# A short causal convolution ahead of a ReGLU feed-forward: VectorE's convolution lane works one unit ahead instead of two

## The chip, the cores and the metric

One NeuronCore of a Trainium2 chip runs one program. The metric is the device time of an execution in microseconds (us); lower is better.

## The reference

`x` is 8 batches x 4096 tokens x 192 channels. Each of 8 heads (24 channels each) has 7 taps, a softmax over `weight`. A causal convolution over the tokens with these taps is followed by a gated feed-forward layer with 1536 hidden columns:

```python
w = softmax(weight, axis=-1)                                  # 8 x 7
out = einsum('hk,bskhg->bshg', w, windows of 7 tokens of x)   # zeros ahead of token 0
x = out.reshape(B * S, 192)
return (maximum(x @ w_gate, 0) * (x @ w_val)) @ w_out         # 192 -> 1536 -> 192
```

## The kernel before

**Units.** Four pairs of batches (batch b and batch b + 4 lie as two streams of 64 rows on the 128 partitions) are cut into units of 1024 tokens: 16 units, `u` = 0 to 15, two windows of 512 tokens in each. For each unit TensorE runs the *gates* (`gate_val`, line 505): two windows, in each 12 slices of hidden columns, in each six pairs of 64-row matmuls. Per slice ScalarE makes the ReLU (line 516) and VectorE the product `hT` (line 517). Then it runs the *projection* (`project`): four pieces of 512 tokens times `Wo`, each copied out by ScalarE (line 573; the last piece of a unit is shared with VectorE) and stored by a DMA on SP's queue (line 574).

**Half passes.** In all units but unit 0 a piece is projected in two turns of `half_pass` (line 528), 48 matmuls of 64 rows each, two of them side by side in the array. The second turn adds into the banks of the first, with the row halves exchanged, so it may start only when the first is over. This is told through an empty instruction on SP:

```python
        if turn == 0:
            done = nc.sync.nop()
            tc.add_manual_dep(done.ins, mm.ins.name, SYNC, reason="first turn over")
```

The first matmul of the second turn waits for this nop (line 549 in the profile). The order of turns is (0,0) (1,0) (0,1) (2,0) (1,1) (3,0) (2,1) (3,1), written (piece, turn). Unit 0 uses `half_whole` (line 553) in place of it: 48 matmuls of 128 rows per piece, with no second turn and no nop.

**Where the convolution is done.** The gates read the convolved tokens `xc[u]`. Unit 0 comes from small TensorE matmuls (`conv_dense`). Unit 1 comes from `conv(2)` and `conv(3)`: eight matmuls with band matrices each, five ScalarE copies into `y` (line 373, `move`), and DMA transposes on SP into `xc[1]` (line 395), five per group. Units 2 to 15 come from the *lane*: `lane_load` (GpSimd's queue loads raw tokens into `x_e`), `lane_turn` (GpSimd copies to `x_p`, nine DMA transposes on SP make `x_r`, line 436), `lane_first` (ScalarE, tap 0, into `acc`, line 469), `lane_rest` (VectorE, taps 1 to 6 on the first 576 tokens, line 481; 18 instructions, the last three write `xc`), `product` (ScalarE line 452 and VectorE line 454, taps times the last 448 tokens) and `add` (GpSimd sums the products, line 458).

**Order.** The schedule is written by hand: each engine runs its instructions in program order. In round `u` of the main loop the lane of unit `u + 2` is turned on GpSimd and SP during the gates, taken by ScalarE and VectorE during the projection, and its sums are added by GpSimd in the next round. PSUM is a ring of four buffers of two banks.

**Start.** GpSimd's queue issues the weight loads, and GpSimd copies slices 2 to 5 of `Wg` and `Wv` to the other 64 partitions (`pool_halves`, line 180); then come the copy of `tap`, `lane_load(2)`, `load_x(2)`, the load of `Wo`, and in round 0 `lane_turn(2)` and `load_x(3)`.

Of the kernel before, what the change touches and what calls it, by code (L numbers as in the profile page):

```python
# [15 lines left out]
def kernel(  # L16
# [41 lines left out]
    second = [min(t, 2 * UNIT - SUB) for t in range(UNIT, 2 * UNIT, SUB)]  # L58
    GROUPS += [(0, second[:GSUB]), (0, second[GSUB:])]
# [3 lines left out]
    xpool = ctx.enter_context(tc.tile_pool(name="xpool", bufs=3))  # L63
# [3 lines left out]
    ypool = ctx.enter_context(tc.tile_pool(name="ypool", bufs=2))  # L67
# [7 lines left out]
    def load_x(g):  # L75


        bp, toks = GROUPS[g]
        xt = xpool.tile([128, GSUB, 2, D], F16, name="x_h")
        rows, step = (SUB, DSUB) if g < 2 else (128, SUB)  # L80
        for st in range(2):
            b = bp + NB * st
            last = toks[-1] - toks[-2] != step
            n_full = len(toks) - int(last)
            src = bass.AP(
                tensor=x.tensor,
                offset=x.offset + (b * S + toks[0] - PAD) * D,
                ap=[[D, rows], [step * D, n_full], [1, D]],
            )
            nc.gpsimd.dma_start(out=xt[0:rows, 0:n_full, st, :], in_=src)  # L90
            if last:
                nc.gpsimd.dma_start(
                    out=xt[0 : SUB + PAD, len(toks) - 1, st, :],
                    in_=x[b, toks[-1] - PAD : toks[-1] + SUB, :],
                )
        return xt

# [87 lines left out]

    load_w(0)
# [5 lines left out]
    load_w(4, 6)  # L192
    pool_halves(3)

# [150 lines left out]
    convs = {}  # L345

    def conv(g, part):


        xt = xts[g]  # L350
        bp, toks = GROUPS[g]
        n = len(toks)
        rows = SUB + PAD
        W = 2 * n * G
        ps = psum.tile([128, 2, 512], FP, name="ps")
        for h, (t, bank, slot) in PLACE.items():
            if t == part:
                nc.tensor.matmul(  # L358
                    out=ps[0:SUB, bank, W * slot : W * (slot + 1)],
                    lhsT=band(h),  # L360
                    rhs=xt[0:rows, 0:n, :, G * h : G * (h + 1)],
                    start=True,
                    stop=True,
                    skip_group_check=True,
                )
        if part == 0:
            convs[g] = ypool.tile([128, GSUB, NCH, 2, 64], F16, name="y")
        y = convs[g]

        def move(copy, bank, i0, step_in, c, r0, step_out, width):  # L370
            src = ps[0:SUB, bank, 0 : 2 * W]
            dst = y[0:SUB, 0:n, 0, :, 0:1]
            copy(
                out=bass.AP(
                    tensor=dst.tensor,
                    offset=dst.offset + 128 * c + r0,
                    ap=[dst.ap[0], [step_out, 2], [NCH * 128, n], [64, 2], [1, width]],
                ),
                in_=bass.AP(
                    tensor=src.tensor,  # L380
                    offset=src.offset + i0,
                    ap=[src.ap[0], [W + step_in, 2], [2 * G, n], [G, 2], [1, width]],
                ),
            )

        if part == 0:
            move(nc.scalar.copy, 0, 0, 0, 0, 0, G, G)
            move(nc.scalar.copy, 1, 0, 0, 1, 8, G, G)
            return
        move(nc.scalar.copy, 0, 0, 0, 2, 16, G, G)  # L390
        move(nc.scalar.copy, 1, 0, 8, 0, 48, 2 * 128 - 48, 16)
        move(nc.scalar.copy, 1, 16, -16, 1, 0, 56, 8)
# [7 lines left out]
    xes, xrs, accs, prods = {}, {}, {}, {}  # L400

    def lane_load(u):


        bp, t0 = u * UNIT // S, u * UNIT % S
        xe = epool.tile([128, TILES, 2, NCH, 64], F16, name="x_e")
        j0 = int(t0 == 0)
        if j0:
            nc.gpsimd.memset(xe[0:HALO, 0, :, :, :], 0.0)
        for st in range(2):  # L410
            b = bp + NB * st
            for j, n in ((j0, TDVE - j0), (TDVE, TILES - TDVE)):
                lo = t0 - HALO + 128 * j if j < TDVE else t0 + LDVE - HALO
                nc.gpsimd.dma_start(  # L414
                    out=xe[:, j : j + n, st, :, :].rearrange("p j c r -> p j (c r)"),
                    in_=bass.AP(
                        tensor=x.tensor,
                        offset=x.offset + (b * S + lo) * D,
                        ap=[[D, 128], [128 * D, n], [1, D]],
                    ),  # L420
                )
            if j0:
                nc.gpsimd.dma_start(
                    out=xe[HALO:128, 0, st, :, :].rearrange("p c r -> p (c r)"),
                    in_=x[b, 0 : 128 - HALO, :],
                )
        xes[u] = xe

    def lane_turn(u):
        xe = xes.pop(u)  # L430
        xp = epool.tile([128, TILES, NCH, 2, 64], F16, name="x_p")
        for st in range(2):
            nc.gpsimd.tensor_copy(out=xp[:, :, :, st, :], in_=xe[:, :, st, :, :])  # L433
        xr = rpool.tile([128, NCH, 128 * TILES], F16, name="x_r")
        for j in range(TILES):
            nc.sync.dma_start_transpose(
                out=xr[:, :, 128 * j : 128 * j + 128],
                in_=xp[:, j].rearrange("p c s r -> p (c s r)"),
            )
        xrs[u] = xr  # L440

    def shifted(u, c, k, lane):
        o = HALO - KW + 1 + k
        if lane:
            return xrs[u][:, c, 128 * TDVE + o : 128 * TDVE + o + LPOOL]
        return xrs[u][:, c, o : o + LDVE]

    def product(engine, u, c, k):
        out = prods[u][:, k, c, :]
        in_, scale = shifted(u, c, k, 1), tap[:, c, k : k + 1]  # L450
# [5 lines left out]
    def add(u, k):  # L456
        pr = prods[u]
        nc.gpsimd.tensor_tensor(  # L458
            out=pr[:, 0] if k < KW - 1 else xc[u][:, :, LDVE:UNIT],
# [5 lines left out]
    def lane_first(u):  # L465
        accs[u] = apool.tile([128, NCH, LDVE], FP, name="acc")
        xc[u] = xcpool.tile([128, NCH, UNIT], F16, name="xc")
        for c in range(NCH):
            nc.scalar.activation(  # L469
                out=accs[u][:, c, :],  # L470
                in_=shifted(u, c, 0, 0),
# [3 lines left out]
        prods[u] = apool.tile([128, KW, NCH, LPOOL], FP, name="prods")  # L475

    def lane_rest(u):
        acc = accs.pop(u)
        for k in range(1, KW):
            for c in range(NCH):  # L480
                nc.vector.scalar_tensor_tensor(  # L481
                    out=xc[u][:, c, 0:LDVE] if k == KW - 1 else acc[:, c, :],
                    in0=shifted(u, c, k, 0),
# [5 lines left out]
        for c, k in VECTOR[u > 2]:  # L489
            product(nc.vector, u, c, k)  # L490
# [35 lines left out]
    SYNC = mybir.DependencyInfo(mybir.DependencyClass.Sync, mybir.DependencyReason.DATA)  # L526

# [24 lines left out]

    def half_whole(h, st, outs):
        for q in range(4):
            for f in range(NFF):
                nc.tensor.matmul(  # L556
                    out=outs[q],
                    lhsT=h[:, f, st, 128 * q : 128 * (q + 1)],
                    rhs=Wo[:, f, :],
                    start=(f == 0),  # L560
                    stop=(f == NFF - 1),
                )
# [45 lines left out]
    def project(u, hs, work):  # L608
# [3 lines left out]
        if u == 0:  # L612
            order = [(i, 2) for i in range(4)]
        if u == NUNIT - 1:
            order = [(0, 0), (1, 0), (0, 1), (2, 0), (1, 1), (2, 1), (3, 2)]
        for i, turn in order:
# [5 lines left out]
            if turn in (0, 2):  # L622
                at[i] = slots()
            if turn in (1, 2):
                for c, k in work[i]:
                    product(nc.scalar, u + 2, c, k)
            if turn == 2:
                half_whole(h, st, at[i][1])
            else:
                done[i] = half_pass(h, st, at[i][1], turn, done.get(i))  # L630
            if turn:
                evict(at[i][0], row0, u > 0 and i == 3 or u == NUNIT - 1 and i == 2)
            if u == 0 and i == 0:
                conv(3, 0)
                conv(3, 1)
# [7 lines left out]
    pool_halves(5)  # L643
    nc.gpsimd.tensor_copy(out=tap[64:128], in_=tap[0:64])
    lane_load(2)
    xts[2] = load_x(2)
    nc.gpsimd.dma_start(out=Wo[:], in_=moe_w_out.rearrange("(c p) d -> p c d", p=128))
    for u in range(NUNIT):
        lane = 1 <= u < NUNIT - 1
        if lane:  # L650
            add(u + 1, 1)
        if u == 1:
            lane_load(3)
            add(2, 2)
            add(2, 3)
# [3 lines left out]
        if u + 2 < NUNIT:  # L659
            lane_turn(u + 2)  # L660
        if u == 0:
            xts[3] = load_x(3)
        if 0 < u < NUNIT - 3:
            lane_load(u + 3)
        if lane:
# [50 lines left out]
```

## Time and profile before

| | |
|---|---|
| Median of 3 runs | 768.06 us (767.74 to 768.5) |
| The profiled execution: its time | 767.88 us |
| Its span, first to last instruction | 765.9 us |
| TensorE busy | 761.7 us (99%) |
| VectorE busy | 692.7 us (90%) |
| ScalarE busy | 600.7 us (78%) |
| GpSimd busy | 369.9 us (48%) |
| Mean granted TensorE clock | 1.000 |

The span is a run of TensorE work from end to end: gates of a unit, projection of a unit, sixteen times. Busy time of another engine counts only where TensorE waits for it. Times below are us from the span's start. Instructions of one engine overlap a little in the records, so a group's length is shorter than the sum of its durations.

### The profile page before, as it was taken

To read this page: it belongs to the slowest core of one execution; us is meant where nothing else is said; L and a number is where in the kernel's file an instruction comes from. 1 tells how busy PE (TensorE), PEld (TensorE's weight loads), DVE (VectorE), ACT (ScalarE), POOL (GpSimd) and SP (SyncE) were. 2 spreads that over 40 slices of the span, in tenths; PEclk is the share of its full clock that TensorE was granted. 3 is DMA by queue.
4 is the path that set the end of the run, shared out by engine and by line. 5 is a ranking of instruction groups with operands and counts; after the bars stand their busy time and mean duration, and the time that the engine had idled before them with its cause. 6 is when DMAs were issued, how large, how long until landed. Compare 5 with 4: busy or idle time off the path is not lost.

```text
span 765.9 us, 24782 instructions
## 1 busy us (share of the span) xinstructions
PE 761.7 (99%) x10794; PEld 502.5 (66%) x10794; DVE 692.7 (90%) x746; ACT 600.7 (78%) x735; POOL 369.9 (48%) x212
## 2 busy tenths in 40 slices
PE   9999999999999999999999999999999999999998
PEld 4595674946749476584755848567484674947648
DVE  7999999999999999999999999999999999996591
ACT  6797887878878787887878878788787887875571
POOL 8608648093570926619166290743908346090000
PEclk9999999999999999999999999999999999999999
DMA  8966727190472804528054281722919131200202
GB/s 121 134 104 116 92 91 88 54 122 6 100 78 66 110 23 97 61 85 95 23 111 47 85 92 44 106 31 85 93 44 117 21 92 39 65 22 15 71 2 84
DMA packets 131810, 56.12 MB, mean 73 GB/s; under 512 B 96741, under 2 KB 131701, under 8 KB 131701
## 3 DMA queue, kind: packets, MB, share of 16 engines
q1 hardware_dynamic: 90789, 38.85, 25.1%
q0 software_dynamic: 40768, 15.59, 18.9%
q8 instruction: 84, 1.38, 0.8%
q14 instruction: 25, 0.20, 0.1%
q10 hardware_dynamic: 144, 0.10, 0.0%
HBM read 31.68 MB, written 25.17 MB: 74 GB/s over the span
## 4 chain that ended last, share of the span: by engine, by line
PE 99%; DMA 1%; issue 0%; POOL 0%; ACT 0%; POOLq 0%
PE ps L505 65%; PE ps L536 31%; PE ps L556 2%; DMA x_h<-in_x_dram 1%; PE ps L594 1%; PE ps L333 0%; PE ps L358 0%; POOL spaced L129 0%; ACT acc L573 0%; POOLq L700 0%
## 5 line engine op out<-in xcount | busy, mean ns | idle before, releaser
L517 DVE TENSOR_TENSOR hT<-gr,ps 128x1024 f16<-128x1024 f16 (+1 forms) x386 | 468.9, 1215 | 37.0 <-ACT gr L516 9.9
L516 ACT ACTIVATE gr<-ps 128x1024 f16<-128x1024 f32 (+1 forms) x386 | 392.9, 1019 | 102.4 <-PE ps L505 100.6
L458 POOL TENSOR_TENSOR prods<-prods 128x1344 f32<-128x1344 f32 x70 | 212.4, 3034 | 309.1 <-DVE prods L454 305.7
L505 PE MATMUL ps<-xc,Wg 64*128 64x512 f16 x2304 | 311.9, 376 | 0.0
L505 PE MATMUL ps<-xc,Wv 64*128 64x512 f16 x2304 | 311.8, 376 | 0.0
L536 PEld LDWEIGHTS <-hT 64*128 64x128 f16 x5664 | 234.1, 94 | 3.6
L536 PE MATMUL ps<-Wo,hT 64*128 64x192 f16 x5664 | 236.1, 243 | 0.0
L505 PEld LDWEIGHTS <-Wv 64*128 64x128 f16 x2304 | 129.8, 94 | 118.5 <-DVE hT L517 0.3
L505 PEld LDWEIGHTS <-Wg 64*128 64x128 f16 x2304 | 112.2, 94 | 132.4 <-issue 0.2
L481 DVE SCALAR_TENSOR_TENSOR acc<-x_r,tap,acc 128x576 f32<-128x576 f16 x210 | 154.3, 811 | 1.6 <-ACT acc L469 1.6
L452 ACT ACTIVATE prods<-x_r,tap 128x448 f32<-128x448 f16 x222 | 130.3, 662 | 0.0
L573 ACT COPY out_s<-ps 128x768 f32<-128x768 f32 (+1 forms) x63 | 45.7, 725 | 52.4 <-PE ps L536 42.5
L414 POOL DMA_DIRECT2D x_e<-in_x_dram x56 | 45.1, 818 | 3.4 <-POOL x_p L433 3.4
L433 POOL COPY x_p<-x_e 128x1728 f16<-128x1728 f16 x28 | 44.7, 1624 | 1.7 <-DMA x_e<-in_x_dram 1.6
L458 POOL TENSOR_TENSOR xc<-prods 128x1344 f16<-128x1344 f32 x14 | 42.4, 3027 | 1.1
L481 DVE SCALAR_TENSOR_TENSOR xc<-x_r,tap,acc 128x576 f16<-128x576 f16 x42 | 31.8, 810 | 0.0
L573 DVE COPY out_s<-ps 128x384 f32<-128x384 f32 x15 | 8.3, 550 | 25.5 <-ACT out_s L573 25.5
L469 ACT ACTIVATE acc<-x_r,tap 128x576 f32<-128x576 f16 x42 | 29.4, 766 | 0.0
L454 DVE TENSOR_SCALAR prods<-x_r,tap 128x448 f32<-128x448 f16 x72 | 27.3, 446 | 0.0
L556 PE MATMUL ps<-Wo,hT 128*128 128x192 f16 x192 | 16.2, 246 | 0.0
L556 PEld LDWEIGHTS <-hT 128*128 128x128 f16 x192 | 15.9, 98 | 0.0
L90 POOL DMA_DIRECT2D x_h<-in_x_dram x6 | 4.9, 825 | 0.0
(54 smaller groups left out, 66.9 us busy)
## 6 DMA issues: line engine op xcount, KB each, us to landing
out_dram<-out_s SPq DMA_DIRECT2D x63, 384.0 KB
x_e<-in_x_dram POOLq DMA_DIRECT2D x34, 192.0 KB, 6.2
x_e<-in_x_dram POOLq DMA_DIRECT2D x22, 240.0 KB, 4.8
x_r<-x_p SPq DMA_TRANSPOSE x126
Wo<-in_moe_w_out_dram POOLq DMA_DIRECT2D x1, 576.0 KB
x_h<-in_x_dram POOLq DMA_DIRECT2D x2, 240.0 KB, 7.6
x_h<-in_x_dram POOLq DMA_DIRECT2D x2, 210.0 KB, 5.1
x_h<-in_x_dram POOLq DMA_DIRECT2D x2, 192.0 KB, 7.6
```

What stands on the lines that cost most here:

```text
L414: nc.gpsimd.dma_start(out=xe[:, j : j + n, st, :, :].rearrange("p j c r -> p j (c r)"), in_=bass.AP(tensor=x.tensor, offset=x.offset + (b ...
L433: nc.gpsimd.tensor_copy(out=xp[:, :, :, st, :], in_=xe[:, :, st, :, :])
L452: engine.activation(out=out, in_=in_, func=ACTF.Copy, scale=scale)
L458: nc.gpsimd.tensor_tensor(out=pr[:, 0] if k < KW - 1 else xc[u][:, :, LDVE:UNIT], in0=pr[:, 0], in1=pr[:, k], op=ALU.add,)
L469: nc.scalar.activation(out=accs[u][:, c, :], in_=shifted(u, c, 0, 0), func=ACTF.Copy, scale=tap[:, c, 0:1],)
L481: nc.vector.scalar_tensor_tensor(out=xc[u][:, c, 0:LDVE] if k == KW - 1 else acc[:, c, :], in0=shifted(u, c, k, 0), scalar=tap[:, c, k : k ...
L505: nc.tensor.matmul(out=pss[i][:, st, :], lhsT=W[64 * st : 64 * st + 64, c, 128 * f : 128 * (f + 1)], rhs=xcb[64 * st : 64 * st + 64, c, WI ...
L516: nc.scalar.activation(out=gr[:, sts], in_=pss[0][:, sts], func=ACTF.Relu)
L517: nc.vector.tensor_tensor(out=h[:, f, sts], in0=gr[:, sts], in1=pss[1][:, sts], op=ALU.mult)
L536: mm = nc.tensor.matmul(out=outs[q], lhsT=h[64 * r : 64 * r + 64, f, st, 128 * q : 128 * (q + 1)], rhs=Wo[64 * r : 64 * r + 64, f, :], sta ...
L556: nc.tensor.matmul(out=outs[q], lhsT=h[:, f, st, 128 * q : 128 * (q + 1)], rhs=Wo[:, f, :], start=(f == 0), stop=(f == NFF - 1),)
L573: one(out=dst[:, step * j : step * j + step], in_=src[:, step * j : step * j + step])
```

## The change

- VectorE's part of a lane (the first 576 tokens) now serves unit `u + 1` in the projection of unit `u`; GpSimd's part (the last 448 tokens) still serves unit `u + 2`. A lane `v` is therefore made of two pieces of `x` (`pieces`): the head of unit `v` and the tail of unit `v + 1`.
- There is a lane 1. Its four loads are spread between the weight copies on GpSimd (two ahead of `pool_halves(3)`, one behind it, one behind `pool_halves(5)`); its copies and transposes stand ahead of and behind the load of `Wo` and `load_x(2)`.
- Unit 1's last 448 tokens come from a single group `conv(2)` with four sub-blocks instead of five; `conv(3)` is gone. The group's matmuls stand behind unit 0's gates; its copies and its four transposes (`conv_out`) stand behind `lane_first(1)` and ahead of unit 0's projection.
- `lane_load(2, last)` waits for the last instruction of `lane_first(1)`.
- Unit 0's projection uses the two turns of `half_pass` like the other units; `half_whole` is gone. The last piece of unit 0 is copied out by ScalarE and VectorE together.
- VectorE's products are five in every unit (seven in unit 0 before); in round 1 GpSimd makes two products itself (`FOR_POOL`). The last unit has a lane on VectorE in round 14, which had none.

The core of the diff:

```diff
-    VECTOR = [
-        [(0, 5), (1, 5), (2, 5), (0, 4), (1, 4), (2, 4), (2, 1)],
-        [(0, 5), (1, 5), (2, 5), (0, 6), (2, 1)],
-    ]
+    VECTOR = [(0, 5), (1, 5), (2, 5), (0, 6), (2, 1)]
+    FOR_POOL = [(1, 6), (2, 6)]
...
-    second = [min(t, 2 * UNIT - SUB) for t in range(UNIT, 2 * UNIT, SUB)]
-    GROUPS += [(0, second[:GSUB]), (0, second[GSUB:])]
+    GROUPS += [(0, list(range(UNIT + LDVE, 2 * UNIT, SUB)))]
...
+    def pieces(v):
+        both = [(0, TDVE, v * UNIT)]
+        if v + 1 < NUNIT:
+            both.append((TDVE, TILES - TDVE, (v + 1) * UNIT + LDVE))
+        return both
+
+    def lane_load(v, hold=None):
+        xe = epool.tile([128, TILES, 2, NCH, 64], F16, name="x_e")
+        xes[v] = xe
+        for j0, n, t in pieces(v):
...
+            for st in range(2):
+                b = bp + NB * st
+                first = nc.gpsimd.dma_start(
...
+                if hold is not None:
+                    tc.add_manual_dep(first.ins, hold.ins.name, SYNC, reason="behind the turns of the lane before")
+                    hold = None
...
+                yield
...
     load_w(4, 6)
+    ahead = lane_load(1)
+    next(ahead)
+    next(ahead)
     pool_halves(3)
+    next(ahead)
...
+    def conv(g):
...
+        wide = [psum.tile([128, 2, 512], FP, name="ps") for _ in range(2)]
+        for h, (t, bank, slot) in PLACE.items():
+            nc.tensor.matmul(
+                out=wide[t][0:SUB, bank, W * slot : W * (slot + 1)],
...
+        return wide
+
+    def conv_out(g, wide):
...
+        move(nc.scalar.copy, 0, 0, 0, 0, 0, 0, G, G)
+        move(nc.scalar.copy, 0, 1, 0, 0, 1, 8, G, G)
+        move(nc.scalar.copy, 1, 0, 0, 0, 2, 16, G, G)
+        move(nc.scalar.copy, 1, 1, 0, 8, 0, 48, 2 * 128 - 48, 16)
+        move(nc.scalar.copy, 1, 1, 16, -16, 1, 0, 56, 8)
         for jj, t in enumerate(toks):
             u, k = t // UNIT, min(SUB, UNIT - t % UNIT)
             nc.sync.dma_start_transpose(
...
+    def lane_turn(v):
+        xe = xes.pop(v)
...
+        for j0, n, _ in pieces(v):
+            for st in range(2):
+                nc.gpsimd.tensor_copy(
+                    out=xp[:, j0 : j0 + n, :, st, :], in_=xe[:, j0 : j0 + n, st, :, :]
                 )
+            for j in range(j0, j0 + n):
+                nc.sync.dma_start_transpose(
...
+            yield
...
         order = [(0, 0), (1, 0), (0, 1), (2, 0), (1, 1), (3, 0), (2, 1), (3, 1)]
-        if u == 0:
-            order = [(i, 2) for i in range(4)]
...
     pool_halves(5)
+    load_rest(ahead)
     nc.gpsimd.tensor_copy(out=tap[64:128], in_=tap[0:64])
-    lane_load(2)
+    between = lane_turn(1)
+    next(between)
+    nc.gpsimd.dma_start(out=Wo[:], in_=moe_w_out.rearrange("(c p) d -> p c d", p=128))
     xts[2] = load_x(2)
-    nc.gpsimd.dma_start(out=Wo[:], in_=moe_w_out.rearrange("(c p) d -> p c d", p=128))
+    load_rest(between)
     for u in range(NUNIT):
...
+        adds = 1 <= u < NUNIT - 1
+        if u + 1 < NUNIT:
+            xc[u + 1] = xcpool.tile([128, NCH, UNIT], F16, name="xc")
+        if adds:
+            add(u, 1)
         hs = []
         if u == 0:
             hs.append(gate_val(0, 0))
...
+        if 0 < u < NUNIT - 1:
+            load_rest(lane_turn(u + 1))
+        if 0 < u < NUNIT - 2:
+            load_rest(lane_load(u + 2))
+        if u == 1:
+            for c, k in FOR_POOL:
+                product(nc.gpsimd, u, c, k)
+        if adds:
+            for k in range(2, KW):
+                add(u, k)
         while len(hs) < 2:
             hs.append(gate_val(u, len(hs)))
...
+        wide = conv(2) if u == 0 else None
+        if u + 1 < NUNIT:
+            last = lane_first(u + 1)
+            if u == 0:
+                conv_out(2, wide)
+                load_rest(lane_load(2, last))
+            lane_rest(u + 1)
         if u + 2 < NUNIT:
...
-            cut = [0, 4, 8, 12, 16] if u == 0 else [0, 5, 10, 15, 16]
-            work = [todo[a:b] for a, b in zip(cut, cut[1:])]
+            work = [todo[a:b] for a, b in zip([0, 5, 10, 15], [5, 10, 15, 16])]
         project(u, hs, work)
```

More of the change, by code (lines that the diff above doesn't have):

```diff
@@ L78, in load_x @@
         bp, toks = GROUPS[g]
+        n, rows, step = len(toks), SUB if g < 2 else 128, toks[1] - toks[0]
         xt = xpool.tile([128, GSUB, 2, D], F16, name="x_h")
-        rows, step = (SUB, DSUB) if g < 2 else (128, SUB)
         for st in range(2):
-            b = bp + NB * st
-            last = toks[-1] - toks[-2] != step
-            n_full = len(toks) - int(last)
             src = bass.AP(
                 tensor=x.tensor,
-                offset=x.offset + (b * S + toks[0] - PAD) * D,
-                ap=[[D, rows], [step * D, n_full], [1, D]],
-            )
[L90 to L95, printed above, removed]
+                offset=x.offset + ((bp + NB * st) * S + toks[0] - PAD) * D,
+                ap=[[D, rows], [step * D, n], [1, D]],
+            )
+            nc.gpsimd.dma_start(out=xt[0:rows, 0:n, st, :], in_=src)
         return xt
+    SYNC = mybir.DependencyInfo(mybir.DependencyClass.Sync, mybir.DependencyReason.DATA)
     xts = {}
@@ L184, in pool_halves, with load_rest @@
         both_halves(nc.gpsimd.tensor_copy, s, Wv)
+    xes, xrs, accs, prods = {}, {}, {}, {}
+    def pieces(v):
[7 more added lines that the diff above has]
+        for j0, n, t in pieces(v):
+            bp, t0 = t // S, t % S
+            start = int(t0 == 0)
+            if start:
+                nc.gpsimd.memset(xe[0:HALO, j0, :, :, :], 0.0)
+            for st in range(2):
+                b = bp + NB * st
+                first = nc.gpsimd.dma_start(
+                    out=xe[:, j0 + start : j0 + n, st, :, :].rearrange("p j c r -> p j (c r)"),
+                    in_=bass.AP(
+                        tensor=x.tensor,
+                        offset=x.offset + (b * S + t0 - HALO + 128 * start) * D,
+                        ap=[[D, 128], [128 * D, n - start], [1, D]],
+                    ),
+                )
+                if hold is not None:
+                    tc.add_manual_dep(first.ins, hold.ins.name, SYNC, reason="behind the turns of the lane before")
+                    hold = None
+                if start:
+                    nc.gpsimd.dma_start(
+                        out=xe[HALO:128, j0, st, :, :].rearrange("p c r -> p (c r)"),
+                        in_=x[b, 0 : 128 - HALO, :],
+                    )
+                yield
+    def load_rest(steps):
+        for _ in steps:
+            pass
     load_w(0)
@@ L343, in conv_dense, with move @@
         copy(out=xc[0][:, c, t0 : t0 + WIN], in_=ps[:, 0, :])
-    convs = {}
-    def conv(g, part):
+    def conv(g):
         xt = xts[g]
+        n = len(GROUPS[g][1])
+        rows = SUB + PAD
+        W = 2 * n * G
+        wide = [psum.tile([128, 2, 512], FP, name="ps") for _ in range(2)]
+        for h, (t, bank, slot) in PLACE.items():
+            nc.tensor.matmul(
+                out=wide[t][0:SUB, bank, W * slot : W * (slot + 1)],
+                lhsT=band(h),
+                rhs=xt[0:rows, 0:n, :, G * h : G * (h + 1)],
+                start=True,
+                stop=True,
+                skip_group_check=True,
+            )
+        return wide
+    def conv_out(g, wide):
         bp, toks = GROUPS[g]
         n = len(toks)
-        rows = SUB + PAD
         W = 2 * n * G
[L355 to L371, printed above, removed]
+        y = ypool.tile([128, GSUB, NCH, 2, 64], F16, name="y")
+        def move(copy, t, bank, i0, step_in, c, r0, step_out, width):
+            src = wide[t][0:SUB, bank, 0 : 2 * W]
             dst = y[0:SUB, 0:n, 0, :, 0:1]
@@ L384, in move @@
             )
[L386 to L392, printed above, removed]
+        move(nc.scalar.copy, 0, 0, 0, 0, 0, 0, G, G)
[3 more added lines that the diff above has]
+        move(nc.scalar.copy, 1, 1, 16, -16, 1, 0, 56, 8)
         for jj, t in enumerate(toks):
@@ L398, in conv @@
             )
[L400 to L420, printed above, removed]
-                )
[L422 to L425, printed above, removed]
-                )
-        xes[u] = xe
@@ L429, in lane_turn @@
[L429 to L440, printed above, removed]
@@ L442, in shifted @@
-    def shifted(u, c, k, lane):
+    def lane_turn(v):
+        xe = xes.pop(v)
+        xp = epool.tile([128, TILES, NCH, 2, 64], F16, name="x_p")
+        xr = rpool.tile([128, NCH, 128 * TILES], F16, name="x_r")
+        xrs[v] = xr
+        for j0, n, _ in pieces(v):
+            for st in range(2):
+                nc.gpsimd.tensor_copy(
+                    out=xp[:, j0 : j0 + n, :, st, :], in_=xe[:, j0 : j0 + n, st, :, :]
+                )
+            for j in range(j0, j0 + n):
+                nc.sync.dma_start_transpose(
+                    out=xr[:, :, 128 * j : 128 * j + 128],
+                    in_=xp[:, j].rearrange("p c s r -> p (c s r)"),
+                )
+            yield
@@ L443, in shifted, with product @@
+    def shifted(v, c, k, lane):
         o = HALO - KW + 1 + k
         if lane:
[L445 to L450, printed above, removed]
+            return xrs[v][:, c, 128 * TDVE + o : 128 * TDVE + o + LPOOL]
+        return xrs[v][:, c, o : o + LDVE]
+    def product(engine, v, c, k):
+        out = prods[v][:, k, c, :]
+        in_, scale = shifted(v, c, k, 1), tap[:, c, k : k + 1]
@@ L454, in product, with add @@
             engine.tensor_scalar(out=out, in0=in_, scalar1=scale, scalar2=None, op0=ALU.mult)
-    def add(u, k):
-        pr = prods[u]
+    def add(v, k):
+        pr = prods[v]
         nc.gpsimd.tensor_tensor(
-            out=pr[:, 0] if k < KW - 1 else xc[u][:, :, LDVE:UNIT],
+            out=pr[:, 0] if k < KW - 1 else xc[v + 1][:, :, LDVE:UNIT],
             in0=pr[:, 0],
@@ L463, in add, with lane_first @@
         )
-    def lane_first(u):
-        accs[u] = apool.tile([128, NCH, LDVE], FP, name="acc")
-        xc[u] = xcpool.tile([128, NCH, UNIT], F16, name="xc")
+    def lane_first(v):
+        accs[v] = apool.tile([128, NCH, LDVE], FP, name="acc")
         for c in range(NCH):
-            nc.scalar.activation(
-                out=accs[u][:, c, :],
-                in_=shifted(u, c, 0, 0),
+            last = nc.scalar.activation(
+                out=accs[v][:, c, :],
+                in_=shifted(v, c, 0, 0),
                 func=ACTF.Copy,
@@ L474, in lane_first, with lane_rest @@
             )
-        prods[u] = apool.tile([128, KW, NCH, LPOOL], FP, name="prods")
-    def lane_rest(u):
-        acc = accs.pop(u)
+        return last
+    def lane_rest(v):
+        acc = accs.pop(v)
         for k in range(1, KW):
@@ L481, in lane_rest @@
                 nc.vector.scalar_tensor_tensor(
-                    out=xc[u][:, c, 0:LDVE] if k == KW - 1 else acc[:, c, :],
-                    in0=shifted(u, c, k, 0),
+                    out=xc[v][:, c, 0:LDVE] if k == KW - 1 else acc[:, c, :],
+                    in0=shifted(v, c, k, 0),
                     scalar=tap[:, c, k : k + 1],
@@ L488, in lane_rest @@
                 )
-        for c, k in VECTOR[u > 2]:
-            product(nc.vector, u, c, k)
+        if v + 1 < NUNIT:
+            prods[v] = apool.tile([128, KW, NCH, LPOOL], FP, name="prods")
+            for c, k in VECTOR:
+                product(nc.vector, v, c, k)
     def gate_val(u, w):
@@ L551, in half_pass @@
             return done
[L553 to L562, printed above, removed]
     def put(copy, queue, src, row, n, gap, os_=None):
@@ L621, in project @@
                 continue
-            if turn in (0, 2):
+            if turn == 0:
                 at[i] = slots()
-            if turn in (1, 2):
+            else:
                 for c, k in work[i]:
[L626 to L630, printed above, removed]
+                    product(nc.scalar, u + 1, c, k)
+            done[i] = half_pass(h, st, at[i][1], turn, done.get(i))
             if turn:
[L632 to L635, printed above, removed]
+                evict(at[i][0], row0, i == 3 or u == NUNIT - 1 and i == 2)
     for c in range(NCH):
@@ L658 @@
             hs.append(gate_val(0, 0))
[L659 to L665, printed above, removed]
-            for k in range(4 if u == 1 else 2, KW - 1):
-                add(u + 1, k)
+        if 0 < u < NUNIT - 1:
[8 more added lines that the diff above has]
+                add(u, k)
         while len(hs) < 2:
             hs.append(gate_val(u, len(hs)))
-        if lane:
-            add(u + 1, KW - 1)
-        if u == 0:
-            xc[1] = xcpool.tile([128, NCH, UNIT], F16, name="xc")
-            conv(2, 0)
-            conv(2, 1)
         del xc[u]
         work = [[] for _ in range(4)]
+        wide = conv(2) if u == 0 else None
[5 more added lines that the diff above has]
+            lane_rest(u + 1)
         if u + 2 < NUNIT:
-            lane_first(u + 2)
-            lane_rest(u + 2)
             todo = [(c, k) for k in (0, 1, 2, 3, 4, 6) for c in range(NCH)]
-            todo = [ck for ck in todo if ck not in VECTOR[u > 0]]
-            cut = [0, 4, 8, 12, 16] if u == 0 else [0, 5, 10, 15, 16]
-            work = [todo[a:b] for a, b in zip(cut, cut[1:])]
+            todo = [ck for ck in todo if ck not in VECTOR + (FOR_POOL if u == 0 else [])]
+            work = [todo[a:b] for a, b in zip([0, 5, 10, 15], [5, 10, 15, 16])]
         project(u, hs, work)
```

12 lines of the change are left out of this document (2 added, 10 removed).

## The prediction

> **What bounds the kernel now.** I read the busy times first, then the chain of waits in order of time, then the timelines of ScalarE and SP around the end of unit 0's gates, then SP's waits.
>
> ```profile
> PE 761.7 (99%) x10794; PEld 502.5 (66%) x10794; DVE 692.7 (90%) x746; ACT 600.7 (78%) x735; POOL 369.9 (48%) x212
> ```
>
> The chain (start, length, what):
>
> ```profile
> 21.57 19.56 PE ps L505 x180
> 41.13 0.99 PE ps L358 x8
> 42.12 3.96 PE ps L556 x48
> 46.09 0.82 PE ps L358 x8
> 46.91 11.88 PE ps L556 x144
> 58.79 31.19 PE ps L505 x288
> 89.97 15.84 PE ps L536 x384
> 105.81 31.08 PE ps L505 x288
> ...
> 387.33 31.08 PE ps L505 x288
> ```
>
> TensorE is the path from end to end: 31.08 us of gates, 15.84 of projection, no gap. Only two things move the end: TensorE work taken out, and a new wait of TensorE. The two groups of `conv` (L358) stand on the path; 192 whole matmuls (3.96 + 11.88 = 15.84) take as long as 384 half ones (15.84).
>
> ScalarE, then SP, in unit 0 (start, length):
>
> ```profile
> 40.52 1.02 ACT L516 ACTIVATE gr<-ps 128x1024 f16<-128x1024 f32 x1 [0.27 <-PE ps L505]
> 41.71 2.00 ACT L373 CAST y<-ps 112x480 f16<-112x480 f32 x5 [0.17 <-PE ps L358]
> 43.57 2.14 ACT L469 ACTIVATE acc<-x_r,tap 128x576 f32<-128x576 f16 x3
> ...
> 47.82 0.81 ACT L573 COPY out_s<-ps 128x768 f32<-128x768 f32 x1
> ```
>
> ```profile
> 43.74 6.92 SPq L395 DMA_TRANSPOSE xc<-y  x5
> 50.76 0.53 SPq L574 DMA_DIRECT2D out_dram<-out_s  x1
> ```
>
> The reader is to see that SP is busy while it issues transposes: five take 6.92 us, and the store of a piece that ScalarE had copied by 47.82 + 0.81 = 48.63 is issued at 50.76, right behind the fifth. In unit 7, with nothing ahead of it, the store follows the copy's end (377.48 + 0.80) at once:
>
> ```profile
> 377.48 0.80 ACT L573 COPY out_s<-ps 128x768 f32<-128x768 f32 x1 [0.78 <-PE ps L536]
> ```
>
> ```profile
> 378.30 0.37 SPq L574 DMA_DIRECT2D out_dram<-out_s  x1
> ```
>
> And SP's waits show that the nop between the turns of a half pass is a real instruction in that queue (59 times, none in unit 0):
>
> ```profile
> SPq L549 <- PE ps L536: 279.1, 59, 31.5
> ```
>
> **The change part by part.** The sum is made against the profiled execution (767.88 us; span 765.9, 1.98 around it), 0.18 below the median of 768.06.
>
> *Taken off TensorE's path.* `conv(3)`: -0.82. `conv(2)` streams 192 columns in place of 240: 8 x 48 / 240 x 0.1025 us = 0.16 less work (0.82 / 8 = 0.1025 each), but its second half waits for VectorE's product of slice 10 (in before 0.99 - 0.82 = 0.17 is that wait) and so starts no earlier: only four matmuls gain, -0.08, end at 42.04. Unit 1's gates take 31.19 against 31.08 elsewhere; their buffers come free in the steady way now, since the last copy of unit 0 is shared: -0.11. Unit 0's projection in half passes: 0. Sum -1.01.
>
> *Added to TensorE's path: the nop behind the transposes.* Unit 0 now has half passes, so turn (0,1) waits for a nop on SP. In program order SP has ahead of it the four transposes of `conv_out`, which wait for ScalarE's last move, which now stands behind `lane_first(1)`. Step by step: the ReLU starts at 40.52 and the next instruction follows 0.92 later (unit 7: 370.89 to 371.81), 41.44; three `acc` take 2.00 at that pace, 43.44; the five moves took 2.00 with five sub-blocks, with four by their rows (480, 320 and 160 elements: 582, 468, 345 ns, so 0.74 ns an element and 3 x 0.51 + 0.42 + 0.32 = 2.28 against 2.56) 2.00 x 2.28 / 2.56 = 1.78, so 45.2. Four transposes at 1.25 (the median) to 1.42 with the occasional long one are 5.0 to 5.7; I take 5.3: the nop passes at 50.5, TensorE goes on at 50.6. It could have gone on at 42.04 + 2 x 1.98 = 46.0. Stall: +4.6. Bounds: 1.17 each (the shortest) and moves done at 45.0 give 49.7 and +3.8; 1.45 each and 45.4 give 51.2 and +5.3. Queued behind the nop on SP are only stores; those behind TensorE's wait are all the rest of unit 0. Nothing gives it back: later units are TensorE alone.
>
> *The lane one unit nearer.* VectorE's result is now needed by the very next gates. In before it ends early enough:
>
> ```profile
> 384.03 2.27 DVE L481 SCALAR_TENSOR_TENSOR xc<-x_r,tap,acc 128x576 f16<-128x576 f16 x3
> ```
>
> The last `xc` ends at 386.30; the gates start at 387.33 in the chain and read the third chunk two pairs (0.43) later: 1.4 us of slack, to 0.1 the same in the units looked at from 2 to 13. Cost 0; with that cover gone, each us late would be paid at up to 15 boundaries. In unit 0 the lane can start at 42.80, when VectorE's last product ends (44.42 before, behind the moves), and ends near 56.1, before 57.9 even without a stall. Unit 15's lane is one more such boundary, without products. VectorE's two products fewer in unit 0: 0.
>
> *The start.* GpSimd issues two `x_e` loads (0.82 each) ahead of `pool_halves(3)`, which in before waited until 13.17 for its weights: its copies now run 13.8 to 15.4 in place of 13.17 to 14.77. TensorE reads them at 14.98 and 15.63: 0.2 to 0.4 of slack, so 0, at most 0.4. Slices 4 and 5 end near 20.0 (19.6 before) for 21.5. `x_p` of lane 1 is 21 to 27, its nine transposes (12.87 in before, 1.43 each) 23 to 36, taken at 41.4 by `acc`: 5 us of cover, 0. `Wo` and `x_h` are issued by 25.7 for 41; the loads of `x_e` took 4.2 to 7.9 to land. The held `lane_load(2)` blocks GpSimd's queue from 27 to 43.4; behind it waits only `add(1, 1)`, which needs VectorE's products at 58. GpSimd's two products in round 1 have no row; between the 768-element copy (0.82) and the 1344-element add (3.03) they cost 1.6 to 6 together, nearer the copy by size: that round's GpSimd work then ends at 58 + 3.0 + 3.4 + 3.3 + 5 x 3.05 + 1.6 to 6, 84.6 to 89, ahead of ScalarE's next products (92.3 before, later with the stall): 0. Four copies in place of two per lane, +0.2 on GpSimd: 0.
>
> Sum: 767.88 - 1.01 + 4.6 = 771.47; with half of the 0.18 to the median, 771.6.
>
> **Rivals.**
> *The clock falls in the stall.* Once work has started, no pause of TensorE in this trace is near 4.6 us, so none shows what follows one. The nearest row is the start, where the first wide matmuls run at half pace:
>
> ```profile
> 2.52 1.16 PE L157 MATMUL ps<-const-bfloat16-1.0 128*128 128x512 bf16 x3
> 2.95 0.74 PE L157 MATMUL ps<-const-bfloat16-1.0 128*128 128x512 bf16 x2
> ...
> 5.15 0.44 PE L157 MATMUL ps<-const-bfloat16-1.0 128*128 128x512 bf16 x2
> ```
>
> Starts of 512-wide ones lie 0.43 apart, against 31.08 / 144 = 0.216 for a pair later; by 5.15 a wide and a narrow one take 0.44 together. Slow from 0.86 to between 4.3 and 5.15, 3.4 to 4.3 us at half pace, costs 1.7 to 2.1: 773.4 in all. Against it: the mean clock is listed as 1.00 even there, so that row can't tell. [...] Chance 0.3.
>
> *The nop doesn't wait* (the other side): SP hands its transposes on and the nop passes by 46.0. Then 767.88 - 1.01 = 766.9, 0.15% below the median, which is within 0.2%, about what a measurement of this kernel can tell from no change. It decides at SP's time per transpose: no stall below 0.2 us each, break-even (nop by 47.0) at 0.45; the shortest of ten in before is 1.17. Against it stands the store at 50.76. Chance 0.09, of which a third is a gain over 0.2% by savings that I don't see.
>
> *The lane misses its deadline*: 1.4 us per unit is all there is. If VectorE's lane were 2 us late at each of 15 boundaries, 0.6 a time is 9 us: 781. For it: it is the one cover that all units share. Against: 18 instructions end at the same offset in every unit, and GpSimd is idle meanwhile, as before. Chance 0.06.
>
> **How the numbers follow.** Stall with full clock, 771.6, 0.55; stall with a slow spell, 773.4, 0.3; no stall 0.09; late lane 0.06. The bounds of the stall make the first 770.8 to 772.3, the slow spell 772.5 to 774.4. The range 770.0 to 774.4 leaves out the last two cases and little else. Slower over 0.2% (above 769.6): 0.90; within: 0.06; faster: 0.04.
>
> **What would show it.** In the profile after: TensorE idle about 4.6 us ahead of the first matmul of turn (0,1), released by SP's nop; SP with four transposes of `y` from about 45.2 to 50.5, the nop at their end; unit 1's gates from about 62.5; each later unit 46.92 again; the half passes behind the stall at 1.98 each (slow spell: the first ones near 4). Wrong: unit 1's gates at 57.9 (no stall), a gap ahead of gates in every unit (late lane), or a wait at slices 5 to 11 of unit 0 for GpSimd's copies.

## The result, and the profile after

| | before | after |
|---|---|---|
| Median | 768.25 us (4 runs, 767.74 to 768.5) | 775.3 us (4 runs, 774.2 to 775.85) |
| Ratio, 95% interval | | 1.009 (1.0074 to 1.0106) |
| Profiled execution: its time, its span | 767.88, 765.9 us | 774.79, 772.8 us |
| Mean granted TensorE clock | 1.000 | 0.996 |

The change made the kernel 7 us slower. The forecast was 771.6, with a range to 774.4: the way was right, the size was not.

From the page of the changed kernel, TensorE's busy time and the granted clock in 40 slices:

```profile
PE 763.5 (99%) x10978; PEld 501.1 (65%) x10978; DVE 705.6 (91%) x763; ACT 600.5 (78%) x733; POOL 377.2 (49%) x242
...
PE   9979999999999999999999999999999999999998
...
PEclk9989999999999999999999999999999999999999
```

TensorE is still busy for 99%, which hides the loss: the third slice (39 to 58 us) is down to seven tenths in the row of PE and to eight in the row of the clock, and time at half clock counts as busy (1.00 of the microsecond from 54.00, at a clock of 0.50). The chain of waits of the changed kernel, in order of time (start, length, what), from unit 0's last gates on:

```profile
43.74 1.57 ACT y L410 x5
45.31 0.02 issue
45.32 1.18 SPq L430
46.50 0.04 issue
46.54 1.25 SPq L430
47.79 0.04 issue
47.84 1.30 SPq L430
49.14 0.04 issue
49.18 1.25 SPq L430
50.43 0.05 issue
50.48 0.02 SPq L558
50.50 0.05 issue
50.55 14.62 PE ps L545 x271
65.17 31.08 PE ps L516 x288
96.25 15.84 PE ps L545 x352
```

The chain, which was TensorE alone before, leaves it here: ScalarE's five copies into `y`, the four transposes on SP, the nop of turn (0,1) (0.02 us long) behind them, and only then the matmuls. TensorE's own waits say the same:

```profile
PE ps L545 <- SPq L558: 4.2, 1, 4.2
```

Six turns of 1.98 us should follow in 11.88 us; they took 14.62. The windows of the profile give the reason (columns: the stretch, its length, busy time of PE, PEld, DVE, ACT and POOL with counts, then the granted clock, the DMA share and GB/s):

```profile
48.75:49.00 0.25, 0.00 (x0) 0.00 (x0) 0.25 (x2) 0.00 (x0) 0.00 (x0) 1.00 1.39 178
49.00:49.25 0.25, 0.00 (x0) 0.00 (x0) 0.25 (x1) 0.00 (x0) 0.00 (x0) 0.63 1.39 178
49.25:49.50 0.25, 0.00 (x0) 0.00 (x0) 0.25 (x2) 0.00 (x0) 0.00 (x0) 0.50 1.42 180
```

```profile
54.00:55.00 1.00, 1.00 (x16) 0.93 (x14) 1.00 (x2) 0.39 (x1) 0.00 (x0) 0.50 0.00 0
55.00:56.00 1.00, 1.00 (x18) 0.94 (x14) 1.00 (x2) 1.00 (x3) 0.00 (x0) 0.55 0.06 16
56.00:57.00 1.00, 1.00 (x30) 1.00 (x26) 1.00 (x4) 1.00 (x3) 0.00 (x0) 1.00 0.56 177
```

Turn (1,0) ended at 46.31. The mean of 0.63 in 49.00 to 49.25 puts the fall to half clock at 49.07, in the middle of the pause; the same arithmetic on the row of 55.00 to 56.00 puts the rise at 55.90. In the microsecond from 54.00, at a clock of 0.50, 16 matmuls run; in the one from 56.00, at 1.00, 30.

The whole difference, along the two chains: unit 0's gates end at 41.33 instead of 41.13, +0.20; `conv(2)` and the first two turns together +0.03 (41.33 to 46.31, against 0.99 + 3.96); the pause +4.24; six turns at partly half clock, 14.62 - 11.88 = +2.74; `conv(3)` gone, -0.82; unit 1's gates 31.08 instead of 31.19, -0.11. That makes +6.28, and the chains end at 763.16 and 769.43. The span ends 3.37 us later than that, with the last store, against 2.74: +0.63. In the other profiles of this study that stretch takes 2.66 to 3.31, so this one is a little above them all, and no run explains it.

### The profile page after: what moved, and what is told of

It reads as the page before. It is cut to its first block, busy times and chain, and to the rows that moved or that the text cites. A ratio compares the mean times of both kernels' runs of the same rounds, so it can differ in the third digit from the quotient of the medians.

```text
span 772.8 us, 25194 instructions
## 1 busy us (share of the span) xinstructions
PE 763.5 (99%) x10978; PEld 501.1 (65%) x10978; DVE 705.6 (91%) x763; ACT 600.5 (78%) x733; POOL 377.2 (49%) x242
## 4 chain that ended last, share of the span: by engine, by line
PE 97%; SPq 1%; ACT 1%; DMA 0%; issue 0%; ACTq 0%
PE ps L516 64%; PE ps L545 32%; SPq L430 1%; PE ps L592 1%; PE ps L370 0%; DMA prods<-in_x_dram 0%; ACT y L410 0%; ACT acc L478 0%; ACT x_h L316 0%; SPq L95 0%; ACT acc L571 0%; ACTq L478 0%; ACT gr L527 0%; SPq L558 0%
## 5 line engine op out<-in xcount | busy, mean ns | idle before, releaser
L545 PE MATMUL ps<-Wo,hT 64*128 64x192 f16 x6048 | 254.8, 244 | 4.2 <-SPq L558 4.2
L545 PEld LDWEIGHTS <-hT 64*128 64x128 f16 x6048 | 252.0, 95 | 8.6 <-SPq L558 4.5
L490 DVE SCALAR_TENSOR_TENSOR acc<-x_r,tap,acc 128x576 f32<-128x576 f16 x225 | 165.3, 812 | 0.0
L571 ACT COPY out_s<-ps 128x768 f32<-128x768 f32 (+1 forms) x63 | 45.2, 718 | 58.8 <-PE ps L545 50.2
L197 POOL DMA_DIRECT2D x_e<-in_x_dram x58 | 47.0, 822 | 20.4 <-ACT acc L478 17.1
L442 POOL COPY x_p<-x_e 128x960 f16<-128x960 f16 (+1 forms) x58 | 50.3, 909 | 0.1
L490 DVE SCALAR_TENSOR_TENSOR xc<-x_r,tap,acc 128x576 f16<-128x576 f16 x45 | 34.0, 811 | 0.0
L478 ACT ACTIVATE acc<-x_r,tap 128x576 f32<-128x576 f16 x45 | 31.4, 764 | 0.0
L148 PE MATMUL ps<-const-bfloat16-1.0 128*128 128x512 bf16 (+1 forms) x10 | 3.9, 526 | 0.8 <-PEq L690 0.8
L370 PEld LDWEIGHTS <-x_h 110*32 110x32 f16 (+3 forms) x240 | 3.2, 92 | 2.2 <-issue 1.3
L370 PE MATMUL ps<-band,x_h 110*32 110x104 f16 (+7 forms) x240 | 4.0, 209 | 0.4 <-ACT x_h L316 0.4
```

What stands on the lines that cost most here:

```text
L197: first = nc.gpsimd.dma_start(out=xe[:, j0 + start : j0 + n, st, :, :].rearrange("p j c r -> p j (c r)"), in_=bass.AP(tensor=x.tensor, off ...
L442: nc.gpsimd.tensor_copy(out=xp[:, j0 : j0 + n, :, st, :], in_=xe[:, j0 : j0 + n, st, :, :])
L478: last = nc.scalar.activation(out=accs[v][:, c, :], in_=shifted(v, c, 0, 0), func=ACTF.Copy, scale=tap[:, c, 0:1],)
L490: nc.vector.scalar_tensor_tensor(out=xc[v][:, c, 0:LDVE] if k == KW - 1 else acc[:, c, :], in0=shifted(v, c, k, 0), scalar=tap[:, c, k : k ...
L545: mm = nc.tensor.matmul(out=outs[q], lhsT=h[64 * r : 64 * r + 64, f, st, 128 * q : 128 * (q + 1)], rhs=Wo[64 * r : 64 * r + 64, f, :], sta ...
L571: one(out=dst[:, step * j : step * j + step], in_=src[:, step * j : step * j + step])
```

## The experiments

Times are medians; the kernel before ran on the same chip in each group (767.9 to 768.0). The first four ran together.

**The transposes behind the first nops.**

```diff
+    AHEAD = 0
+    later = []
...
-        for jj, t in enumerate(toks):
...
+        def turns(some):
+            for jj, t in list(enumerate(toks))[some]:
...
+        turns(slice(0, AHEAD))
+        later.append(lambda: turns(slice(AHEAD, None)))
...
             done[i] = half_pass(h, st, at[i][1], turn, done.get(i))
+            if u == 0 and (i, turn) == (1, 0):
+                later.pop()()
```

> The four transposes of y are issued on SP behind the nops of turns (0,0) and (1,0) instead of ahead of them; all else is as in the changed kernel. Theory (the nop waits behind the transposes, and TensorE's clock falls in the pause): no pause, no slow clock, so what is left is conv(3) gone (-0.8), unit 1's buffers (-0.1) and up to +0.2 at the start: 767.4 us, 0.9 under the kernel before. Rival (half passes in unit 0, the nearer deadline of the lane or the loads at the start cost the time): still 774 to 775.

768.45 us (11 runs, 767.29 to 770.1), ratio 1.0001 (0.9992 to 1.001). The 7 us are gone and the mean clock is 0.999 or 1.000, so nothing else in the change costs them. The rest is 1 us over the expectation. Part of that is in unit 0's chain of the profiled execution (769.31 us), whose gates also end 0.43 later than in the kernel before (41.56 against 41.13):

```profile
42.48 12.48 PE ps L551 x299
54.95 1.44 issue
56.39 3.70 PE ps L551 x85
```

TensorE stood still for 1.44 us inside turn (2,1), on nothing that the profile shows.

**Matmuls in the pause.**

```diff
             done[i] = half_pass(h, st, at[i][1], turn, done.get(i))
+            if u == 0 and (i, turn) == (1, 0):
+                idle = psum.tile([128, 2, 512], FP, name="ps")
+                for n in range(19):
+                    nc.tensor.matmul(
+                        out=idle[:, n % 2, :], lhsT=busy[:, 0:128], rhs=busy[:], start=True, stop=True
+                    )
```

> Nineteen matmuls of 512 columns that nobody reads stand between turn (1,0) and turn (0,1) of unit 0; the nop still waits behind the transposes. They take about 4.1 us, the length of the pause. Theory: the wait stays (4.2 us), the granted clock stays at 1.00, and the 2.7 us that the half passes lost at half clock are gone: 772.5 us. Rival (the half passes behind the pause are slow for another reason, such as DMA traffic or banks): 775.

771.48 us (4 runs, 771.36 to 771.8), 1.0 under the expectation, clock 1.000 in every execution. Its chain:

```profile
42.21 4.07 PE ps L545 x96
46.27 0.32 PE ps L627
46.59 0.06 issue
46.65 3.88 PE ps L627 x17
50.53 12.04 PE ps L545 x288
62.57 31.08 PE ps L516 x288
```

The six turns start at the same moment as in the changed kernel (50.53 and 50.55), with much the same DMA traffic beside them (a share of 1.50 and 1.47 from 50 to 52 us), and take 12.04 instead of 14.62 us. So the wait is one thing, the slow turns another, and what makes them slow is that TensorE stood idle. This is the kernel that tells the two apart: 768 + 3.6 with the wait alone, 775 with the clock's fall.

**Two of the four transposes ahead of the nops** (`turns(slice(0, 2))` at once, the rest behind turn (1,0)).

> Two of the four transposes stand ahead of the nops, two behind. Theory: the nop passes two transposes earlier (2.55 us), the pause is 1.7 us, and that is too short for the clock to fall: 767.4 + 1.7 = 769.1 us, clock 1.00 throughout. If the clock falls in a pause of 1.7 us too: 771 to 772.

769.58 us (10 runs, 769.1 to 770.96). In the profiled execution the pause is 1.6 us and the turns behind it run at full pace, six in 12.05:

```profile
46.33 1.25 SPq L433
47.58 0.05 issue
47.63 0.02 SPq L564
47.65 0.04 issue
47.69 12.05 PE ps L551 x288
```

Four of the ten executions list a mean clock of 0.999, the others 1.000. Kernels without a pause list 0.999 now and then too (one of 27 executions of the kernel before, two of 11 with the nops first), so a short fall in some executions is neither shown nor ruled out.

**Whole matmuls in unit 0** (`half_whole` as in the kernel before).

> Unit 0 is projected with whole matmuls as in the kernel before (no second turn, no nop); all else as in the changed kernel, the transposes in their place. Theory: the same as with the nops first, 767.4 us. Rival (the transposes themselves, or the lane's deadline, slow TensorE without the nop): 770 or more.

767.32 us (10 runs, 767.02 to 768.75), ratio 0.9992 (0.9983 to 1.0001). The four transposes stand where the change has them (45.21 to 50.35 on SP) and cost nothing, since no turn waits for SP.

The second four:

**Three of the four transposes ahead.**

> Three of the four transposes stand ahead of the nops of unit 0, one behind: the pause of TensorE should be about 2.9 us, between the 1.6 of two ahead and the 4.2 of four. [...]

771.89 us (4 runs, 770.47 to 772.35). The forecast was 767.3 + 2.9 = 770.2 us if the clock stays up, and 771.5 to 773.5 if it falls in some or all executions. The profiled execution (771.73 us) has the pause but full clock:

```profile
PE ps L551 <- SPq L564: 2.9, 1, 2.9
...
PE ps L522 <- POOL Wg L173: 0.4, 1, 0.4
```

The other three have mean clocks of 0.997, 0.998 and 0.999; 0.997 of some 770 us is 0.003 x 770 / 0.5 = 4.6 us at half clock, an estimate. No execution of a kernel without a pause lists less than 0.999, so the clock probably fell in two executions, in the profiled one it did not, and the fourth can't be told. That speaks for a fall in some executions. The time alone does not: the profiled execution came into the range of a fall without one, because its `conv(2)` starts 1.2 us later than in the kernel before (42.28 against 41.06). The second line is a part of that cost, which comes up again below.

**No hold on the load of lane 2**, once with the nops first and once with whole matmuls (`load_rest(lane_load(2))` without `last`).

> As the kernel with the nops first (768.45 us, spread 767.29 to 770.1), but lane_load(2) does not wait for lane_first(1): its four loads are issued from about 27 us, ahead of the end of unit 0's gates, beside the transposes of lane 1. Theory (the 1.44 us in which TensorE waited for nothing that the profile shows, 55 to 56.4, is its instructions arriving late behind those loads and the transposes): the gap and the spread go, 767.2 us. Rival (the gap has another cause): still 768.4 with a spread of 3 us. If the loads delay the transposes of lane 1 past 41.6 us, unit 0's lane starts late: over 768.5.

768.48 us (11 runs, 767.16 to 769.13). There is no gap in unit 0's projection in this profile, but the median is no better, so the theory that these loads cost the time isn't borne out; what made the gap stays open. What is late in this execution is the start, where TensorE waits for GpSimd's copy of `Wg`:

```profile
PE ps L522 <- POOL Wg L173: 0.6, 1, 0.6
```

> Whole matmuls in unit 0 (767.32 us) and no hold on lane_load(2). If the hold only keeps loads away from transposes that have time to spare: 767.2 us, the same as with the hold. If it protects lane 1's transposes: later.

767.59 us (11 runs, 766.95 to 768.26), ratio 0.9992 (0.9983 to 1.0001), the same as with the hold. The hold neither costs nor protects anything that these runs show.

**The transposes behind the whole projection of unit 0**, half passes and hold kept.

> Half passes in unit 0, the hold kept, and the four transposes of y issued behind the whole projection of unit 0 on SP (about 58 us; unit 1's second window reads them at 73). Theory: no pause, clock 1.00, 767.2 us, 0.7 under the kernel before. If the gap of the kernel with the nops first comes from the loads alone and not from the transposes beside them: it stays, 768.4 us with a spread.

767.6 us (11 runs, 767.32 to 769.21), ratio 0.9994 (0.9985 to 1.0003). No gap, but 0.4 over the expectation, and the chain has unit 0's slices 5 and 6 at 2.94 us where the kernel before has 2.70.

The last four, after the waits for GpSimd's weight copies had come up in several profiles:

**Lane 1's loads later at the start**, on top of the kernel with the transposes last.

```diff
     ahead = lane_load(1)
-    next(ahead)
-    next(ahead)
     pool_halves(3)
     next(ahead)
...
     pool_halves(4)
+    next(ahead)
     pool_halves(5)
     load_rest(ahead)
```

> As the kernel with the turns last (767.6 us, 767.32 to 769.21), but lane 1's loads stand later at the start: one behind pool_halves(3), one behind pool_halves(4), two behind pool_halves(5), so that no load is issued between the weights and the copies that TensorE reads at slices 5 and 6. Theory (of the 1.0 us that the smaller TensorE work saves, about 0.4 is given back at the start, because the weight copies run later and TensorE waits for them in many executions): 767.1 us with a narrower spread. Rival (the delays at the start are those of every execution, whatever the loads): 767.6 with the same spread.

767.21 us (11 runs, 766.76 to 768.26), ratio 0.9989 (0.9981 to 0.9998). The chain of this kernel, with no wait for GpSimd left:

```profile
14.87 2.70 PE ps L520 x24
...
40.95 0.91 PE ps L391 x8
41.87 15.95 PE ps L549 x384
57.81 31.08 PE ps L520 x288
```

Unit 1's gates start at 57.81, 0.98 ahead of the kernel before (58.79). It is the only kernel of the study whose interval lies under 1, by little: 0.1% faster than the kernel before, 7 to 8 us faster than the changed one.

**The early loads alone, in the kernel before**: its first lane's four loads moved to the places that the change gives them.

> The kernel before, with one thing moved: the four loads of its first lane (lane 2) stand where the changed kernel has lane 1's (two ahead of pool_halves(3), one behind it, one behind pool_halves(5)). Theory (that place costs): 768.3 to 768.5 us, 0.4 over the kernel before, with a wider spread. Rival: 768.0, no change.

768.38 us (12 runs, 767.76 to 769.7) against 767.91, ratio 1.0006 (0.9998 to 1.0015). The median is 0.47 higher as expected, but the interval takes in no change, and in the profiled execution (767.89 us) slices 5 and 6 take 2.70 as before.

**Whole matmuls with the later loads.**

> Whole matmuls in unit 0 (767.32 us) with lane 1's loads in the later places. Theory: 767.0 us, the best of these kernels, 0.9 under the kernel before. Rival: 767.3 to 767.6.

767.17 us (11 runs, 766.84 to 768.72), ratio 0.9992 (0.9983 to 1.0). Hardly different from 767.32, and its profile still shows slices 5 and 6 late:

```profile
14.91 3.19 PE ps L514 x24
```

Here TensorE's weight loads waited 0.4 and 0.3 us for GpSimd's copies of `Wv` and `Wg`, with no load of lane 1 ahead of `pool_halves(3)`. So the place of the loads can't be the only cause of late copies.

**The changed kernel again.**

> The changed kernel as it is, once more, on the chip of the three above. [...]

774.5 us (4 runs, 774.17 to 776.64), clocks 0.998, 0.995, 0.996 and 0.996: with the first four, the clock fell in all eight executions. The forecast was 774 to 776 us and 0.995 to 0.997 in each execution, with a fall 1 to 4 us after the last matmul and half clock for about 6.8 us. In this profile the fall came later than in the first. TensorE goes on at 51.34 and runs at full clock; the fall comes at 52.24, 5.1 us after the last matmul ahead of the pause, and the rise at 55.65:

```profile
51.90:52.20 0.30, 0.30 (x14) 0.30 (x10) 0.30 (x1) 0.00 (x0) 0.00 (x0) 1.00 0.86 73
52.20:52.30 0.10, 0.10 (x8) 0.10 (x4) 0.10 (x1) 0.00 (x0) 0.00 (x0) 0.69 0.32 49
52.30:52.50 0.20, 0.20 (x8) 0.19 (x4) 0.20 (x2) 0.00 (x0) 0.00 (x0) 0.50 1.16 152
...
55.60:55.70 0.10, 0.10 (x6) 0.09 (x4) 0.10 (x1) 0.10 (x1) 0.00 (x0) 0.75 0.00 0
```

```profile
51.34 13.71 PE ps L545 x288
```

Half clock lasted 3.4 us here, not the expected 6.8 of the first profile. Against the 12.04 us that six turns take at full clock in this place, they lost 1.67 here (13.71) and 2.58 in the first profile (14.62). This execution (774.53 us) is 2.9 us longer than the profiled one with matmuls in the pause (771.6): 1.67 is the clock, 0.86 was lost at the start (`conv(2)` starts at 42.08 instead of 41.22), and 0.42 more lies behind the last copy.

## Why the prediction was wrong, point by point

**The stall: right.** The nop was to pass at 50.5 and TensorE to go on at 50.6; it was 50.48 and 50.55. The transposes ran from 45.32 to 50.43 (predicted 45.2 to 50.5). The pause was 4.24 and not 4.6, since turn (1,0) ended at 46.31 and not at 46.0. The match of the end points has some luck in it: `acc` started 0.20 late (41.64), and the copies (1.57 for 1.78) and the transposes (5.11 for 5.3) were shorter than in the sum. That the queue's order is the cause is shown by the nops first, by no nop at all and by the transposes last, which have no pause, and by two and three transposes ahead, with pauses of 1.6 and 2.9 us.

**The clock: the step that failed.** The sum runs the turns behind the stall at full clock, 1.98 us each, and adds nothing for the clock. The fall was only a rival, with a chance of 0.3 and a price of 1.7 to 2.1 us. The chance was the author's estimate: no trace of the kernel before shows what follows such a pause. The fall happened in all eight executions and cost 2.58 and 1.67 in the two that were profiled. The rival's length, worked out from the start of the kernel as 3.4 to 4.3 us, was 6.8 where the fall came inside the pause (49.07 to 55.90) and 3.4 in the second profile (52.24 to 55.65). The moment differed too: in the first profile 2.76 us after the last matmul, with TensorE idle, in the second after 0.9 us of new work (51.34 to 52.24). What sets the moment and the length was not shown.

**What the fall doesn't cover.** Without the fall the forecast's own working gives 771.5, and the kernel with matmuls in the pause measured 771.48. So close a match is partly luck: a stall put 0.34 too long (4.26 there) stands against 0.11 of savings too many (below) and 0.16 at the start (its gates end at 41.29, 41.13 before). The profiled execution of the changed kernel was put at 771.47 and took 774.79, 3.32 more: the six turns +2.74, the stretch behind the last copy +0.63, the start +0.20, `conv(2)` with the first two turns +0.11, the stall -0.36. In the second profile the clock's 1.67 is the lower end of the rival's price; most of the rest of its 774.53 was lost at the start and behind the last copy. Why other executions took up to 776.64 isn't known.

**`conv(3)` and `conv(2)`: right; unit 1's gates: no saving.** `conv(3)` is -0.82 as said, and `conv(2)` took 0.91 or 0.92 in eight of the other profiles, 0.08 less, as said. Unit 1's gates do take 0.11 less, but not for the reason given (the shared last copy): the kernel with whole matmuls shares that copy, and its unit 1 still takes 31.19. With half passes unit 0's projection takes 15.95 instead of 15.84, so projection and gates together take 47.03 either way. The 0.11 only moves, and the sum of the savings should have been 0.90, not 1.01.

**The nearer deadline of the lane: right.** Every later unit but the last takes 31.08 + 15.84 in the changed kernel's chain, and the last takes 31.08 + 11.88 + 4.08, as before.

**The start: undersized.** It was put at 0, at most 0.4, on 0.2 to 0.4 of slack. The first profile of the changed kernel lost 0.09 at slices 5 and 6, but others lost up to 0.49 there (3.19 against 2.70), and in the first kernel without the hold a copy came so late that TensorE stood for 0.6. In the second profile of the changed kernel, where a copy of `Wv` stood on the chain at 19.04, behind weights that landed at 18.99, `conv(2)` started 1.02 later than in the kernel before (42.08 against 41.06). With the loads later the median fell by 0.4 between two groups, and the early loads alone raised it by 0.47, an interval that just takes in zero. So of the 0.9 us that the change was worth in TensorE work, somewhat under half was probably given back there; this is supported, not settled.

**The chances.** The four cases add up to 0.91 for slower and 0.03 for faster, not to 0.90 and 0.04.

**Open:** the gap of 1.44 us in the first experiment. It was seen in one profile, beside the highest DMA share of that stretch (2.71 from 54 to 55 us), and in none of the other kernels' profiles.

## What to carry to other kernels

An instruction that does nothing still took its place in SP's queue here, behind 5.1 us of transposes. Before a wait is routed through an engine, list what that engine issues ahead of it, and for how long each holds it. When a stall of TensorE is added up, add what its clock does after a pause: with the slow turns, the pause of 4.2 us cost 6.8 and 5.9 us in the two profiles, and the one of 1.6 cost no more than itself in its profile. Filling a pause that can't be removed with matmuls nobody reads is a cheap test, and took 3 us or more off the changed kernel's median here.

## What the runs showed of the hardware that was not expected

- A DMA transpose of 112 x 384 elements held SP's queue for 1.18 to 1.30 us (four in a row), and a nop behind them waited for all of them.
- After a pause of 4.2 us TensorE's granted clock was 0.50 for 6.8 us in one profile and 3.4 us in another. Where it fell inside the pause, the fall came 2.76 us after the last matmul; in the other it came 0.9 us after work had begun again.
- A pause of 1.6 us left the clock at 1.00 in the profiled execution; so did one of 2.9 us, but two other executions with it list mean clocks of 0.997 and 0.998.
- With 19 matmuls that nobody reads in the pause, the clock was 1.000 in all four executions.
